# Two more Strassen groups in the last two chunks, one Silu moved, and the last stores on other queues

## Chip, cores and metric

The kernel runs on one core of a Trainium2 chip. The metric is the device time of one execution, in microseconds (us). A profiled execution also has a span, from its first recorded instruction to its last, which is a little shorter than its time.

## The reference, cut to what matters

The inputs are q, k and v (8 batches, 8 heads, 576 positions, 64 features), a matrix w_in (512 x 2048) and w_out (2048 x 512), all fp32. A softmax-weighted linear attention gives x, 4608 tokens by 512 features, and a two-layer network follows:

```
kv  = einsum('bhsd,bhse->bhde', softmax_seq(k), v)
att = einsum('bhsd,bhde->bhse', softmax_feat(q), kv)
x   = att.transpose(0, 2, 1, 3).reshape(4608, 512)
h   = x @ w_in                       # the first product
g   = h * (1 / (1 + exp(-h)))        # Silu
out = g @ w_out                      # the second product
```

## The kernel before, in words

**Tiling.** The 4608 tokens are nine chunks of 512, t = 0 to 8. XT (two tiles, by the parity of t) holds x transposed, GT (two tiles) holds g transposed: 2048 features as 16 blocks of 128 on the partitions, tokens along the free axis. W1 and W2 hold the weights in fp16. Matmuls write PSUM tile PS, 8 banks of 512 fp32. ACT (ScalarE) and DVE (VectorE) read the banks out. SP, POOL and in a few places ACT issue DMAs.

**The first product.** Up to chunk 1 every block is plain. From chunk 2 on, blocks 0 to 3 and 8 to 11 are plain "p" units (`mm1`, matmul at line 274): four matmuls of 512 columns into one of banks 0 to 3, then one Silu of 512 (line 291) or a Tanh and a DVE operation (lines 246 and 247). Blocks 12 to 15 and 4 to 7 are made together in Strassen's form, in Winograd's variant: seven "g" units (`group`, line 362) in the order 1, 2, 6, 5, 7, 4, 3, each of 8 matmuls of 256 columns. Units 1, 6, 7 and 4 accumulate in banks 0 and 1, units 2, 5 and 3 in banks 2 and 3. Four sums of weights (`ws_op`, line 316, WS1 to WS4) are made once, near 40 us, and four sums of the chunk's x (`xs_op`, line 325) once a chunk, on DVE. Between units come:

- snapshots, `group_snap` (ACT, line 338), copies of banks 0 and 1 to the tiles h0, h1 and h2 after units 1, 6 and 7;
- adds, `group_add` (DVE, line 341), of banks 2 and 3 to such a tile: add 0 after unit 2, add 2 after unit 7, add 1 after unit 3;
- Silus, `group_silu` (ACT, line 347), each of 1024 a partition: one from PSUM after unit 4, and after unit 3 those from h2, h0 and h1, called silu 2, silu 0 and silu 1. Silu 1 waits for add 1.

A unit that overwrites or adds to a bank waits until the bank has been read: unit 6 waits for the first snapshot, units 5 and the next group's unit 2 for adds on banks 2 and 3.

**The second product** of chunk t - 1 runs beside the first of chunk t, wholly in Strassen's form: 14 "b" units (`prod`, line 460), two halves of products 1, 2, 6, 5, 7, 4, 3, each of 8 matmuls of 256 columns into banks 4 and 5. Its sums of g are `s_op` (DVE, line 434, S1 to S4). After some products, `after` takes a snapshot (ACT, line 476, "sa", "sb", "sc") or combines a snapshot with a bank (DVE, lines 480 and 491) into an output tile ow, which SP stores (line 394). The last chunk's second product stands alone at the end (`end`): products 1, 6 and 7 in bank 3, product 2 in bank 5; `part` combines and stores strips of 128 rows by 256 columns in two halves (lines 669 and 684).

**The order** is written out by hand. `units` is the list of PE's work, one unit after the other; `plan(u, f)` puts other work ahead of unit u. An engine's queue has the order in which the code issues instructions, and a waiting instruction holds all behind it. A chunk from 2 to 7 has the units `pbpbpbpbpbpbpbp` and then `ggbgbgbgbbgbgb`; chunk 8 has the two strings the other way round. Attention for a later batch (exponentials on ACT, sums on DVE, products on POOL, `kv_both` and `xt` on PE) is planned between; from chunk 7 on only `xt` for chunk 8 is left of it. `xt` has two halves, each four small matmuls into banks 6 and 7 and a copy to XT, the first half's on DVE, the second's on ACT.

Of the kernel before, what the change touches and what calls it, by code (L numbers as in the profile page):

```python
# [17 lines left out]
def kernel(  # L18
# [9 lines left out]
    nc = tc.nc  # L28
# [32 lines left out]
    T4 = glob.tile([128, HF, HN], FP16, name="T4")  # L61
    GTS = [glob.tile([128, NFB, S], FP16, name="GT0"), glob.tile([128, NFB, TCH], FP16, name="GT1")]
    SS = {i: glob.tile([128, HF, HT], FP16, name=f"S{i}") for i in (1, 2, 4)}
    WS = [glob.tile([128, 2, 512], FP16, name=f"WS{i + 1}") for i in range(4)]
    XS4 = [glob.tile([128, 2, HT], FP16, name=f"XS{i + 1}") for i in range(4)]
    XTS = [glob.tile([128, NC, S], FP16, name=f"XT{i}") for i in range(2)]
    vaug = glob.tile([128, J, NG, E1], BF16, name="vaug")
    ek = glob.tile([128, J, NG * D], BF16, name="ek")
    kvn = [glob.tile([128, 2, 2, D], BF16, name=f"kvn{i}") for i in range(3)]
    ident_f = glob.tile([128, 128], FP32, name="ident_f")  # L70
    ident = glob.tile([128, 128], BF16, name="ident")
    warm = glob.tile([128, 512], BF16, name="warm")
    gate = glob.tile([1, 1], FP32, name="gate")
    dummy = glob.tile([1, 1], FP32, name="dummy")
    PS = ps.tile([128, 8, 512], FP32, name="PS")

    B11, B12 = W2[:, 0:HF, 0:HN], W2[:, 0:HF, HN:DM]
    B21, B22 = W2[:, HF:NFB, 0:HN], W2[:, HF:NFB, HN:DM]
    T3 = B12
# [37 lines left out]

    def qsum_pair(b, cc):
        e = half(st[b]["eq"], cc)
        t1 = ap.tile([128, J, 2, D // 2], FP32, name="t1")  # L120
        t2 = ap.tile([128, J, 2, D // 4], FP32, name="t2", bufs=2)
        nc.gpsimd.tensor_tensor(
            out=t1, in0=e[:, :, :, 0:D // 2], in1=e[:, :, :, D // 2:D], op=ALU.add
        )
        nc.gpsimd.tensor_tensor(
            out=t2, in0=t1[:, :, :, 0:D // 4], in1=t1[:, :, :, D // 4:D // 2], op=ALU.add
        )
        st[b]["t2", cc] = t2
# [157 lines left out]
    def mm1(t, fb, one=False):  # L286
        bank = hb[0] % hb[1]
        hb[0] += 1
        mm1_mm(t, fb, bank, range(NC))
        if one:  # L290
            nc.scalar.activation(  # L291
                out=GTS[t % 2][:, fb, 0:TCH], in_=PS[:, bank, :], func=ACT.Silu, scale=1.0 / XS
            )
        else:
            mm1_silu(t, fb, bank)
# [1 line left out]

    F0, F1 = 12, 4  # L300
    H = [None] * 3

    def wa(c, f):
        return W1[:, 2 * c:2 * c + 2, f * 128:(f + 4) * 128]

    def xb(t, c, n):
        return XTS[t % 2][:, 2 * c:2 * c + 2, (1 - n) * HT:(2 - n) * HT]

    def ws_op(i):
        in0, in1, op = {  # L310
            1: (wa(0, F1), wa(1, F1), ALU.add),
            2: (WS[0], wa(0, F0), ALU.subtract),
            3: (wa(0, F0), wa(0, F1), ALU.subtract),
            4: (wa(1, F0), WS[1], ALU.subtract),
        }[i]
        nc.vector.tensor_tensor(out=WS[i - 1], in0=in0, in1=in1, op=op)

    def xs_op(t, i):
        in0, in1 = {
# [25 lines left out]
    def group_silu(t, i, f, n):  # L345
        x = group_bank(0) if i is None else four(H[i])
        nc.scalar.activation(out=group_out(t, f, n), in_=x, func=ACT.Silu, scale=1.0 / XS)  # L347

    def group(t, i):
        bank = 0 if i in (1, 6, 7, 4) else 2  # L350
        a, bb = {
            1: (wa(0, F0), xb(t, 0, 0)),
            2: (wa(1, F0), xb(t, 1, 0)),
            3: (WS[3], xb(t, 1, 1)),
            4: (wa(1, F1), XS4[3]),
            5: (WS[0], XS4[0]),
            6: (WS[1], XS4[1]),
            7: (WS[2], XS4[2]),
        }[i]
        for p in range(4):  # L360
            for c in range(2):
                nc.tensor.matmul(  # L362
                    out=PS[:, bank + p // 2, (p % 2) * HT:(p % 2 + 1) * HT],
                    lhsT=a[:, c, p * 128:(p + 1) * 128],
                    rhs=bb[:, c, :],
                    start=(i in (1, 2, 5) and c == 0 and p % 2 == 0),
                    stop=(i in (2, 3, 4) and c == 1 and p % 2 == 1),
                    skip_group_check=True,
                )
        if i == 1:  # L370
            group_snap(0)
        elif i == 2:
            group_add(0)
        elif i == 6:
            group_snap(1)
        elif i == 7:
            group_snap(2)
            group_add(2)
        elif i == 4:
            group_silu(t, None, F1, 0)  # L380
        elif i == 3:
            group_silu(t, 2, F1, 1)
            group_silu(t, 0, F0, 0)
            group_add(1)
            group_silu(t, 1, F0, 1)


    def rows(t, col):
# [36 lines left out]
    def s_op(t, i, f0=0, f1=HF):  # L425
        in0, in1, op = {
            1: (blk(t, 0, 1), blk(t, 1, 1), ALU.add),
            2: (SS[1], blk(t, 0, 0), ALU.subtract),
            3: (blk(t, 0, 0), blk(t, 0, 1), ALU.subtract),
            4: (blk(t, 1, 0), SS[2], ALU.subtract),  # L430
        }[i]
        f = slice(f0, f1)
        o = blk(t, 0, 1) if i == 3 else SS[i]
        nc.vector.tensor_tensor(out=o[:, f], in0=in0[:, f], in1=in1[:, f], op=op)
# [170 lines left out]
    def plan(u, f):  # L605
        at.setdefault(u, []).append(f)
# [14 lines left out]
    def b_units(t, order):  # L621
        got = []
        for i in order:
            got.append(lambda t=t, i=i: prod(t, i, 0))

            def second(t=t, i=i):
                prod(t, i, 1)
                after(t, i)

            got.append(second)  # L630
        return got
# [8 lines left out]
    for t in range(2, NCH):  # L640
        begin[t] = len(units)
        bs = b_units(t - 1, ORDER)
        ps_ = [
            lambda t=t, i=i, fb=fb: mm1(t, fb, i < 3 or t + 1 >= B)
            for i, fb in enumerate((0, 8, 1, 9, 2, 10, 3, 11))
        ]
        gs = [lambda t=t, i=i: group(t, i) for i in (1, 2, 6, 5, 7, 4, 3)]
        plan(begin[t] + 2, lambda t=t: s_op(t - 1, 1))
        plan(begin[t] + 4, lambda t=t: s_op(t - 1, 2))
        plan(begin[t] + (15 if t < NCH - 1 else 5), lambda t=t: s_op(t - 1, 3))  # L650
        plan(begin[t] + 21, lambda t=t: s_op(t - 1, 4))
        mix = "pbpbpbpbpbpbpbp", "ggbgbgbgbbgbgb"
        for x in "".join(mix) if t < NCH - 1 else "ggbgbgbgbbgbgb" + "pbpbpbpbpbpbpbp":
            units.append({"p": ps_, "b": bs, "g": gs}[x].pop(0))
        assert not (ps_ or bs or gs)
        x = begin[t] + (1 if t < NCH - 1 else 0)
        plan(x, lambda t=t: (xs_op(t, 1), xs_op(t, 2), xs_op(t, 3), xs_op(t, 4)))


# [7 lines left out]
    def part(name, bank, th, n, a):  # L667
        o = w_out_tile(last, th)[:, a, n * HN:(n + 1) * HN]
        nc.vector.scalar_tensor_tensor(  # L669
            out=o,  # L670
            in0=PS[:, bank, a * HN:(a + 1) * HN],
            scalar=OS,
            in1=WG[last][name][:, a * HN:(a + 1) * HN],
            op0=ALU.mult,
            op1=ALU.add,
        )
        one, two = {
            (0, 0): (nc.sync, nc.sync),
            (1, 1): (nc.gpsimd, nc.gpsimd),
            (1, 0): (nc.sync, nc.scalar),  # L680
            (0, 1): (nc.sync, nc.scalar),
        }[th, n]
        for i, eng in enumerate((one, two)):
            eng.dma_start(  # L684
                out=rows(last, th * HT + a * 128 + i * P)[:, n * HN:(n + 1) * HN],
                in_=o[i * P:(i + 1) * P, :],
            )
# [51 lines left out]
    plan(b1 + 8, lambda: xt(1, 0))  # L739
    plan(b1 + 9, lambda: xt(1, 1))  # L740

    plan(b1 + 3, lambda: (ws_op(1), ws_op(2)))
    plan(b1 + 9, lambda: (ws_op(3), ws_op(4)))
    plan(b1 + 8, lambda: t_op(1, nc.vector, 0, 4))
    plan(b1 + 9, lambda: t_op(1, nc.vector, 4, 8))
    for i, x in enumerate((10, 12)):
# [19 lines left out]
    for t in range(2, NCH - 1):  # L766
        b = t + 1
        u = begin[t]
        if b < B:
            for i in range(2):  # L770
                plan(u + 5 + i, lambda i=i, b=b: exp_q(b, i))
                plan(u + 6 + 3 * i, lambda i=i, b=b: (qsum(b, i), qnorm(b, i, nc.gpsimd)))
                plan(u + 10 + 2 * i, lambda i=i, b=b: vcast(b, i, nc.gpsimd))
                plan(u + 17 + 2 * i, lambda i=i, b=b: exp_k(b, i))
                if b + 1 < B:
                    plan(u + 7 + i, lambda i=i, b=b: load(b + 1, "qt", q, i, nc.sync))
                    plan(u + 18 + i, lambda i=i, b=b: load(b + 1, "vt", v, i, nc.sync))
                    plan(u + 20 + i, lambda i=i, b=b: load(b + 1, "kt", k, i, nc.sync))
            plan(u + 13, lambda b=b: q_transpose(b))
            plan(u + 22, lambda b=b: kv_both(b))  # L780
        plan(u + 24, lambda t=t: xt(t + 1, 0, nc.vector))
        plan(u + 27, lambda t=t: xt(t + 1, 1))

    for u, f in enumerate(units):
        for g in at.get(u, ()):
# [33 lines left out]
```

The softmax here doesn't subtract the row's maximum and nothing guards it: scores larger than these inputs give would overflow.

## Time and profile before

| | us |
|---|---|
| median of three runs | 271.5 |
| lowest and highest | 271.32, 272.15 |
| the profiled run, and its span | 271.31, 269.4 |
| PE busy | 260.4 |
| DVE busy | 190.6 |
| ACT busy | 180.1 |
| chunk 7 starts with its first plain unit at | 200.10 |
| chunk 8 starts with its first group unit at | 226.08 |
| the end starts at | 252.73 |
| DVE's last operation ends at | 265.58 |

The shares say which engine is the longest; the waits of that engine say where its gaps are. The timeline lists instructions in order of start: the start in us from the beginning of the span, the duration, the engine (PEld is the load of weights into TensorE), the line, the operation, the tile written and the tiles read, the shape, and in brackets the engine's idle time before it with what ended that. Neighbours of one kind are merged, with their number at the end (x8). Two starts of PE units are a unit's length apart; durations of a merged PE row are longer by the pipeline's filling.

### The profile page before, as it was taken

To read this page: it belongs to the slowest core of one execution; us is meant where nothing else is said; L and a number is where in the kernel's file an instruction comes from. 1 tells how busy PE (TensorE), PEld (TensorE's weight loads), DVE (VectorE), ACT (ScalarE), POOL (GpSimd) and SP (SyncE) were. 2 spreads that over 40 slices of the span, in tenths; PEclk is the share of its full clock that TensorE was granted. 3 is DMA by queue.
4 is the path that set the end of the run, shared out by engine and by line. 5 is a ranking of instruction groups with operands and counts; after the bars stand their busy time and mean duration, and the time that the engine had idled before them with its cause. 6 is when DMAs were issued, how large, how long until landed. Compare 5 with 4: busy or idle time off the path is not lost.

```text
span 269.4 us, 6058 instructions
## 1 busy us (share of the span) xinstructions
PE 260.4 (97%) x2540; PEld 184.6 (69%) x2540; DVE 190.6 (71%) x269; ACT 180.1 (67%) x228; POOL 71.1 (26%) x62
## 2 busy tenths in 40 slices
PE   8999999999999999999999999999999999999893
PEld 2467644445678767876787678767876787876682
DVE  2966796978898759775977597759776057835432
ACT  5767937669957886788668966896685538484210
POOL 1744971820181008100820082007300000000003
PEclk9999999999999999999999999999999999999999
DMA  7999999499549845994498449830434004200714
GB/s 251 319 209 351 253 339 331 160 256 391 201 124 246 263 113 140 223 300 83 162 283 242 86 156 255 269 74 0 90 65 93 0 2 97 61 0 2 157 43 117
DMA packets 35500, 45.88 MB, mean 170 GB/s; under 512 B 16208, under 2 KB 20048, under 8 KB 35472
## 3 DMA queue, kind: packets, MB, share of 16 engines
q1 hardware_dynamic: 29568, 33.69, 45.1%
q0 software_dynamic: 5584, 11.54, 16.4%
q8 instruction: 20, 0.33, 0.5%
q10 hardware_dynamic: 320, 0.26, 0.3%
q14 instruction: 8, 0.07, 0.1%
HBM read 36.70 MB, written 9.44 MB: 171 GB/s over the span
## 4 chain that ended last, share of the span: by engine, by line
PE 71%; DVE 15%; ACT 8%; issue 3%; DMA 1%; POOL 1%; DVEq 0%
PE PS L460 29%; PE PS L274 16%; PE PS L362 14%; DVE zq L144 5%; DVE GT L247 4%; PE PS L398 3%; PE PS L254 3%; ACT eq L108 3%; PE PS L224 2%; PE PS L185 2%; DVE eq L153 2%; ACT sg L246 2%; ACT L108 2%; DMA qt<-in_q_dram 1%; DVE ow L480 1%
## 5 line engine op out<-in xcount | busy, mean ns | idle before, releaser
L274 PE MATMUL PS<-XT,W 128*128 128x512 f16 (+1 forms) x288 | 71.2, 373 | 0.3 <-ACT ow L410 0.3
L460 PEld LDWEIGHTS <-GT 128*128 128x128 f16 x512 | 49.6, 98 | 13.9 <-issue 2.2
L153 POOL TENSOR_TENSOR eq<-eq,rzq 128x1152 bf16<-128x1152 bf16 x13 | 27.5, 2116 | 105.1 <-DVE rzq L148 105.1
L460 PE MATMUL PS<-W,GT 128*128 128x256 f16 x384 | 49.1, 273 | 0.7 <-ACT GT L291 0.7
L247 DVE SCALAR_TENSOR_TENSOR GT<-sg,PS 128x512 f16<-128x512 f32 (+2 forms) x57 | 37.4, 671 | 10.4 <-ACT sg L246 9.7
L246 ACT ACTIVATE sg<-PS 128x512 f32<-128x512 f32 (+2 forms) x57 | 33.1, 595 | 16.9 <-PE PS L274 8.1
L460 PEld LDWEIGHTS <-S 128*128 128x128 f16 x384 | 37.6, 98 | 8.8
L274 PEld LDWEIGHTS <-W 128*128 128x128 f16 x288 | 27.9, 98 | 21.3 <-issue 1.3
L341 DVE TENSOR_TENSOR h<-PS,h 128x1024 f32<-128x1024 f32 x21 | 25.7, 1221 | 21.3 <-ACT h L338 12.2
L460 PE MATMUL PS<-T,S 128*128 128x256 f16 x256 | 32.7, 273 | 0.0
L338 ACT COPY h<-PS 128x1024 f32<-128x1024 f32 x21 | 21.3, 1012 | 16.3 <-PE PS L362 16.3
L291 ACT ACTIVATE GT<-PS 128x512 f16<-128x512 f32 x31 | 18.5, 595 | 13.3 <-PE PS L274 12.7
L144 DVE TENSOR_REDUCE zq<-eq 128x18 f32<-128x1152 bf16 x12 | 16.2, 1349 | 15.0 <-ACT eq L108 15.0
L362 PEld LDWEIGHTS <-WS 128*128 128x128 f16 x224 | 21.0, 98 | 4.3 <-issue 1.8
L362 PE MATMUL PS<-XS,WS 128*128 128x256 f16 x168 | 21.8, 273 | 0.4 <-ACT h L338 0.4
L684 POOL DMA_DIRECT2D out_dram<-ow x4 | 2.2, 550 | 72.2 <-DVE ow L669 72.2
L347 ACT ACTIVATE GT<-h 128x1024 f16<-128x1024 f32 x21 | 20.7, 1052 | 0.0
L108 ACT ACTIVATE eq<-qt 128x1152 bf16<-128x1152 f32 x16 | 18.1, 1159 | 2.4 <-DMA qt<-in_q_dram 2.3
L362 PEld LDWEIGHTS <-W 128*128 128x128 f16 x168 | 16.4, 98 | 4.5 <-issue 1.4
L111 ACT ACTIVATE ek<-kt 128x1152 bf16<-128x1152 f32 x16 | 18.6, 1164 | 1.2 <-DMA kt<-in_k_dram 1.2
L91 POOL CAST vaug<-vt 128x1152 bf16<-128x1152 f32 x12 | 19.4, 1647 | 0.0
L254 PE MATMUL PS<-XT,W 128*128 128x288 f16 x128 | 16.5, 286 | 0.7 <-DVE GT L247 0.4
(78 smaller groups left out, 337.5 us busy)
## 6 DMA issues: line engine op xcount, KB each, us to landing
out_dram<-ow SPq DMA_DIRECT2D x64, 128.0 KB, 2.4
qt<-in_q_dram SPq DMA_DIRECT2D x12, 576.0 KB, 4.4
kt<-in_k_dram SPq DMA_DIRECT2D x12, 576.0 KB, 8.1
vt<-in_v_dram SPq DMA_DIRECT2D x12, 576.0 KB, 6.4
qt<-in_q_dram POOLq DMA_DIRECT2D x4, 576.0 KB, 13.2
kt<-in_k_dram POOLq DMA_DIRECT2D x4, 576.0 KB, 13.7
vt<-in_v_dram POOLq DMA_DIRECT2D x4, 576.0 KB, 12.6
W<-in_moe_w_out_dram POOLq DMA_DIRECT2D x4, 512.0 KB, 15.1
```

The costliest lines, as they stand in the source:

```text
L108: nc.scalar.activation(out=half(st[b]["eq"], cc), in_=jgd(b, "qt", cc), func=ACT.Exp)
L144: nc.vector.reduce_sum(out=z, in_=e, axis=AX.X)
L153: eng.tensor_tensor(out=e, in0=e, in1=r[:, :, :, None].to_broadcast([128, J, 2, D]), op=ALU.mult)
L246: nc.scalar.activation(out=s, in_=i, func=ACT.Tanh, scale=OS)
L247: nc.vector.scalar_tensor_tensor(out=o, in0=s, scalar=1.0, in1=i, op0=ALU.add, op1=ALU.mult)
L254: nc.tensor.matmul(out=PS[:, 2 * (fb % 3) + n, 0:S // 2], lhsT=W1[:, c, fb * 128:(fb + 1) * 128], rhs=XTS[0][:, c, n * (S // 2):(n + 1) * ...
L274: nc.tensor.matmul(out=PS[:, bank, o0:TCH], lhsT=W1[:, c, fb * 128:(fb + 1) * 128], rhs=XTS[t % 2][:, c, o0:TCH], start=(c == 0), stop=(c ...
L338: nc.scalar.copy(out=H[i], in_=PS[:, 0:2, :].rearrange("p b n -> p (b n)"))
L341: nc.vector.tensor_tensor(out=H[i], in0=PS[:, 2:4, :].rearrange("p b n -> p (b n)"), in1=H[i], op=ALU.add)
L347: nc.scalar.activation(out=group_out(t, f, n), in_=x, func=ACT.Silu, scale=1.0 / XS)
L362: nc.tensor.matmul(out=PS[:, bank + p // 2, (p % 2) * HT:(p % 2 + 1) * HT], lhsT=a[:, c, p * 128:(p + 1) * 128], rhs=bb[:, c, :], start=(i ...
L460: nc.tensor.matmul(out=PS[:, bank, m * HN:(m + 1) * HN], lhsT=a[:, fc, m * 128:(m + 1) * 128], rhs=bb[:, fc, :], start=(first and fc == 0) ...
```

## The change

- In chunks 7 and 8 all 16 blocks of the first product are in Strassen's form. `group` gets an index g: g = 1 for blocks 12 to 15 with 4 to 7, as before, and g = 0 for blocks 8 to 11 with 0 to 3. Both chunks have the units `ggbgbgbgbbgbgb` twice, g = 1 first, and no p units. Both sets use the same sums of x, banks and h tiles.
- Four more WS tiles for g = 0. They are filled on DVE in chunk 7: two operations planned at its unit 8, two at its unit 11.
- In every chunk, silu 1 leaves the end of `group` and is planned three units after group unit 3; in the last group of all, one unit after. Two groups that join, or a group and the p units of the next chunk, so have the next unit's snapshot or Silu on ACT ahead of silu 1.
- S3 of the chunk before is planned at unit 5 of chunk 7 too (it was at 15), and the two halves of `xt` one unit earlier in chunk 7, which has 28 units now and had 29.
- For room: `warm` is the tile XS1, the identity in fp32 is in h0, t1 in h0, and t2 in h1 and h2.
- Last stores: of a strip's two halves, the four of the fourth quadrant stay on POOL and the four of the first on SP. Those of product 4 go ACT and SP (were SP and ACT). Those of product 3 were SP and ACT for both strips; the first strip's now go on ACT and POOL, the last strip's both on SP.

```diff
-    WS = [glob.tile([128, 2, 512], FP16, name=f"WS{i + 1}") for i in range(4)]
+    WS = [[glob.tile([128, 2, 512], FP16, name=f"WS{i + 1}_{g}") for i in range(4)] for g in range(2)]
...
-    ident_f = glob.tile([128, 128], FP32, name="ident_f")
+    ident_f = mp.tile([128, 2 * TCH], FP32, name="h0", bufs=1)[:, 0:128]
...
-    warm = glob.tile([128, 512], BF16, name="warm")
+    warm = XS4[0].rearrange("p a n -> p (a n)")
...
-    def group(t, i):
+    def group(t, g, i):
         bank = 0 if i in (1, 6, 7, 4) else 2
+        w, f0, f1 = WS[g], 4 * g + 8, 4 * g
...
         elif i == 3:
-            group_silu(t, 2, F1, 1)
-            group_silu(t, 0, F0, 0)
+            group_silu(t, 2, f1, 1)
+            group_silu(t, 0, f0, 0)
             group_add(1)
-            group_silu(t, 1, F0, 1)
...
+        free = t + 1 >= B
         ps_ = [
-            lambda t=t, i=i, fb=fb: mm1(t, fb, i < 3 or t + 1 >= B)
-            for i, fb in enumerate((0, 8, 1, 9, 2, 10, 3, 11))
+            lambda t=t, i=i, fb=fb: mm1(t, fb, i < 3)
+            for i, fb in enumerate(() if free else (0, 8, 1, 9, 2, 10, 3, 11))
         ]
...
-        plan(begin[t] + (15 if t < NCH - 1 else 5), lambda t=t: s_op(t - 1, 3))
+        plan(begin[t] + (5 if free else 15), lambda t=t: s_op(t - 1, 3))
...
-        mix = "pbpbpbpbpbpbpbp", "ggbgbgbgbbgbgb"
-        for x in "".join(mix) if t < NCH - 1 else "ggbgbgbgbbgbgb" + "pbpbpbpbpbpbpbp":
+        four_pairs = "ggbgbgbgbbgbgb"
+        for x in (four_pairs if free else "pbpbpbpbpbpbpbp") + four_pairs:
             units.append({"p": ps_, "b": bs, "g": gs}[x].pop(0))
+            if x == "g" and len(gs) % 7 == 0:
+                later = 1 if t == NCH - 1 and not gs else 3
+                f0 = 8 if free and not gs else 12
+                plan(len(units) - 1 + later, lambda t=t, f0=f0: group_silu(t, 1, f0, 1))
...
-            (1, 0): (nc.sync, nc.scalar),
-            (0, 1): (nc.sync, nc.scalar),
+            (1, 0): (nc.scalar, nc.sync),
+            (0, 1): (nc.scalar, nc.gpsimd) if a == 0 else (nc.sync, nc.sync),
...
-        plan(u + 24, lambda t=t: xt(t + 1, 0, nc.vector))
-        plan(u + 27, lambda t=t: xt(t + 1, 1))
+        if b == B:
+            plan(u + 8, lambda: (ws_op(1, 0), ws_op(2, 0)))
+            plan(u + 11, lambda: (ws_op(3, 0), ws_op(4, 0)))
+        plan(u + (24 if b < B else 23), lambda t=t: xt(t + 1, 0, nc.vector))
+        plan(u + (27 if b < B else 26), lambda t=t: xt(t + 1, 1))
```

More of the change, by code (lines that the diff above doesn't have):

```diff
@@ L119, in qsum_pair @@
         e = half(st[b]["eq"], cc)
-        t1 = ap.tile([128, J, 2, D // 2], FP32, name="t1")
-        t2 = ap.tile([128, J, 2, D // 4], FP32, name="t2", bufs=2)
+        t1 = mp.tile([128, 2 * TCH], FP32, name="h0", bufs=1)[:, 0:J * D]
+        t1 = t1.rearrange("p (j g d) -> p j g d", g=2, d=D // 2)
+        t2 = mp.tile([128, 2 * TCH], FP32, name=f"h{cc + 1}", bufs=1)[:, 0:J * D // 2]
+        t2 = t2.rearrange("p (j g d) -> p j g d", g=2, d=D // 4)
         nc.gpsimd.tensor_tensor(
@@ L295, in mm1 @@
             mm1_silu(t, fb, bank)
-    F0, F1 = 12, 4
     H = [None] * 3
@@ L307, in xb, with ws_op @@
         return XTS[t % 2][:, 2 * c:2 * c + 2, (1 - n) * HT:(2 - n) * HT]
-    def ws_op(i):
+    def ws_op(i, g):
+        w, f0, f1 = WS[g], 4 * g + 8, 4 * g
         in0, in1, op = {
[L311 to L314, printed above, removed]
+            1: (wa(0, f1), wa(1, f1), ALU.add),
+            2: (w[0], wa(0, f0), ALU.subtract),
+            3: (wa(0, f0), wa(0, f1), ALU.subtract),
+            4: (wa(1, f0), w[1], ALU.subtract),
         }[i]
-        nc.vector.tensor_tensor(out=WS[i - 1], in0=in0, in1=in1, op=op)
+        nc.vector.tensor_tensor(out=w[i - 1], in0=in0, in1=in1, op=op)
     def xs_op(t, i):
@@ L347, in group_silu @@
         nc.scalar.activation(out=group_out(t, f, n), in_=x, func=ACT.Silu, scale=1.0 / XS)
-    def group(t, i):
+    def group(t, g, i):
         bank = 0 if i in (1, 6, 7, 4) else 2
+        w, f0, f1 = WS[g], 4 * g + 8, 4 * g
         a, bb = {
[L352 to L358, printed above, removed]
+            1: (wa(0, f0), xb(t, 0, 0)),
+            2: (wa(1, f0), xb(t, 1, 0)),
+            3: (w[3], xb(t, 1, 1)),
+            4: (wa(1, f1), XS4[3]),
+            5: (w[0], XS4[0]),
+            6: (w[1], XS4[1]),
+            7: (w[2], XS4[2]),
         }[i]
@@ L379, in group @@
         elif i == 4:
-            group_silu(t, None, F1, 0)
+            group_silu(t, None, f1, 0)
         elif i == 3:
-            group_silu(t, 2, F1, 1)
-            group_silu(t, 0, F0, 0)
+            group_silu(t, 2, f1, 1)
+            group_silu(t, 0, f0, 0)
             group_add(1)
-            group_silu(t, 1, F0, 1)
     def rows(t, col):
@@ L642 @@
         bs = b_units(t - 1, ORDER)
+        free = t + 1 >= B
         ps_ = [
-            lambda t=t, i=i, fb=fb: mm1(t, fb, i < 3 or t + 1 >= B)
-            for i, fb in enumerate((0, 8, 1, 9, 2, 10, 3, 11))
-        ]
-        gs = [lambda t=t, i=i: group(t, i) for i in (1, 2, 6, 5, 7, 4, 3)]
+            lambda t=t, i=i, fb=fb: mm1(t, fb, i < 3)
+            for i, fb in enumerate(() if free else (0, 8, 1, 9, 2, 10, 3, 11))
+        ]
+        gs = [
+            lambda t=t, g=g, i=i: group(t, g, i)
+            for g in ((1, 0) if free else (1,))
+            for i in (1, 2, 6, 5, 7, 4, 3)
+        ]
         plan(begin[t] + 2, lambda t=t: s_op(t - 1, 1))
         plan(begin[t] + 4, lambda t=t: s_op(t - 1, 2))
-        plan(begin[t] + (15 if t < NCH - 1 else 5), lambda t=t: s_op(t - 1, 3))
+        plan(begin[t] + (5 if free else 15), lambda t=t: s_op(t - 1, 3))
         plan(begin[t] + 21, lambda t=t: s_op(t - 1, 4))
-        mix = "pbpbpbpbpbpbpbp", "ggbgbgbgbbgbgb"
-        for x in "".join(mix) if t < NCH - 1 else "ggbgbgbgbbgbgb" + "pbpbpbpbpbpbpbp":
+        four_pairs = "ggbgbgbgbbgbgb"
+        for x in (four_pairs if free else "pbpbpbpbpbpbpbp") + four_pairs:
             units.append({"p": ps_, "b": bs, "g": gs}[x].pop(0))
+            if x == "g" and len(gs) % 7 == 0:
+                later = 1 if t == NCH - 1 and not gs else 3
+                f0 = 8 if free and not gs else 12
+                plan(len(units) - 1 + later, lambda t=t, f0=f0: group_silu(t, 1, f0, 1))
         assert not (ps_ or bs or gs)
-        x = begin[t] + (1 if t < NCH - 1 else 0)
+        x = begin[t] + (0 if free else 1)
         plan(x, lambda t=t: (xs_op(t, 1), xs_op(t, 2), xs_op(t, 3), xs_op(t, 4)))
@@ L740 @@
     plan(b1 + 9, lambda: xt(1, 1))
-    plan(b1 + 3, lambda: (ws_op(1), ws_op(2)))
-    plan(b1 + 9, lambda: (ws_op(3), ws_op(4)))
+    plan(b1 + 3, lambda: (ws_op(1, 1), ws_op(2, 1)))
+    plan(b1 + 9, lambda: (ws_op(3, 1), ws_op(4, 1)))
     plan(b1 + 8, lambda: t_op(1, nc.vector, 0, 4))
```

## The prediction

> **What bounds the kernel now.** I read four views in this order: the shares of the page, busy time by stage, who waited for whom on PE, and the timeline around those waits. The share first:
>
> ```profile
> PE 260.4 (97%) x2540; PEld 184.6 (69%) x2540; DVE 190.6 (71%) x269; ACT 180.1 (67%) x228; POOL 71.1 (26%) x62
> ```
>
> PE is busy for 97%, so the run is as long as PE's work plus its few gaps. Busy time of the engines in three stretches, which are chunk 7, chunk 8, and the end (columns: stretch, its length, then busy us and instructions by engine):
>
> ```profile
> 200.10:226.08 25.98, 25.98 (x209) 19.53 (x207) 13.28 (x17) 14.22 (x20) 0.00 (x0) 1.00 0.20 42
> 226.08:252.73 26.65, 25.57 (x202) 19.54 (x200) 14.78 (x20) 15.26 (x21) 0.00 (x0) 1.00 0.25 54
> 252.73:269.45 16.72, 12.39 (x112) 10.86 (x111) 6.75 (x12) 1.79 (x3) 2.18 (x4) 0.99 0.40 96
> ```
>
> DVE (third engine) is half idle in the two chunks that change, and POOL does nothing there. PE's waits from 180 us on are only two:
>
> ```profile
> PE PS L460 <- ACT GT L291: 0.7, 1, 0.7
> PE PS L362 <- ACT h L338: 0.4, 1, 0.4
> ```
>
> The second is at the start of chunk 8, where one group follows another (start, duration, engine, line; in brackets the idle time before):
>
> ```profile
> 225.35 2.95 ACT L347 ACTIVATE GT<-h 128x1024 f16<-128x1024 f32 x3
> 225.41 1.23 DVE L341 TENSOR_TENSOR h<-PS,h 128x1024 f32<-128x1024 f32 x1 [1.26 <-PE PS L362]
> 226.08 1.91 PE L362 MATMUL PS<-XT,W 128*128 128x256 f16 x16
> ...
> 227.83 1.04 PE L460 MATMUL PS<-W,GT 128*128 128x256 f16 x8
> ...
> 228.20 1.01 ACT L338 COPY h<-PS 128x1024 f32<-128x1024 f32 x1
> ...
> 229.26 1.03 PE L362 MATMUL PS<-XS,WS 128*128 128x256 f16 x8 [0.40 <-ACT h L338]
> ...
> 232.75 1.04 PE L362 MATMUL PS<-XS,WS 128*128 128x256 f16 x8
> ...
> 234.87 1.22 DVE L341 TENSOR_TENSOR h<-PS,h 128x1024 f32<-128x1024 f32 x1 [0.87 <-ACT h L338]
> ...
> 235.37 1.04 PE L362 MATMUL PS<-XS,W 128*128 128x256 f16 x8
> 236.01 0.68 DVE L480 SCALAR_TENSOR_TENSOR ow<-PS,sa 128x512 f32<-128x512 f32 x1
> ```
>
> Group 6 was due one unit after the 227.83 product, at 227.83 + 0.87 = 228.70, and began at 229.26: the wait costs **0.56 us**, the listed 0.40 and the refilling of the pipeline. It waited for the snapshot at 228.20, which stood behind three Silus on ACT. The first wait is the join to the end stage:
>
> ```profile
> 240.60 1.03 PE L274 MATMUL PS<-XT,W 128*128 128x512 f16 x4
> ...
> 251.02 1.03 PE L274 MATMUL PS<-XT,W 128*128 128x512 f16 x4
> ...
> 252.08 0.60 ACT L291 ACTIVATE GT<-PS 128x512 f16<-128x512 f32 x1 [1.14 <-PE PS L274]
> ...
> 252.73 3.65 PE L460 MATMUL PS<-W,GT 128*128 128x256 f16 x32 [0.69 <-ACT GT L291]
> ```
>
> The last plain block starts at 251.02, is through in 0.87, its Silu starts 0.2 later, and the end's product 1 follows 0.05 after that Silu because it writes the same bank 3. It was due at 251.89: **0.84 us** lost. I use these two release times, 0.2 from a PE unit's end to DVE or ACT, 0.05 from DVE or ACT to PE.
>
> **What the Trainium skill says.** "TensorE: Matmul & The Clock Gate", section Back-to-back issue gap, gives N/2.4 + 2.5 ns at full clock: 109 ns for 256 columns, 216 ns for 512, so a Strassen unit of 8 x 256 has no penalty against 4 x 512. The trace agrees: from 240.60 to 251.02 are six pairs of one plain and one product unit, 1.737 us a pair; from 229.26 to 235.37 are seven units of 256 columns, **0.872 us** each; so a plain unit is 1.737 - 0.872 = **0.865 us**. "VectorE: DVE Perf Modes", The perf-mode tier table, lets tensor_tensor run at double rate on 16-bit SBUF data and at single rate with PSUM; here 2048 f16 from SBUF (the S operations, 1.22) and 1024 f32 from PSUM (L341, 1.22) indeed cost the same. "SBUF — State Buffer", Who interferes with whom, says that a DVE instruction with two SBUF inputs contends with a GpSimd one that reads SBUF. The trace before shows the four WS operations once each:
>
> ```profile
> L316 DVE TENSOR_TENSOR WS<-W x2: 685/1102/1520, 37.1 to 41.9; 128x1024 f16<-128x1024 f16 x2
> ...
> L316 DVE TENSOR_TENSOR WS<-WS,W x1: 692/692/692, 38.7 to 38.7; 128x1024 f16<-128x1024 f16 x1
> L316 DVE TENSOR_TENSOR WS<-W,WS x1: 685/685/685, 42.5 to 42.5; 128x1024 f16<-128x1024 f16 x1
> ```
>
> Three took 0.69 us; the one at 37.1 took 1.52, while POOL copied a GT piece. POOL has no work in chunks 7 and 8, so I take 0.69 and keep 1.52 as the upper end.
>
> **The change, part by part.** Sums are against the profiled span, 269.45 us; that execution took 271.31, the others 271.32 to 272.15, their median 271.5, and I subtract from the median.
>
> (1) PE work. In each of chunks 7 and 8, 8 plain units (8 x 0.865 = 6.92) give way to 7 group units (7 x 0.872 = 6.10): -0.82, twice, **-1.64**.
>
> (2) The deferred Silu. At the join of two groups ACT has silus 2 and 0, then the snapshot, then silu 1. The three Silus begin about 0.95 apart, so without the third the snapshot starts at about 227.2 instead of 228.20 and ends 228.2, before 228.70. The 0.56 goes: **-0.56**. In chunks 2 to 6 the same move puts silu 1 behind a plain block's Silu; its values are first read by product 2, four units on, and four PSUM banks rotate, so nothing: hidden behind PE's b units.
>
> (3) New WS operations for blocks 8 to 11 and 0 to 3, in DVE's queue in chunk 7. This is the cost I could not leave at nothing. Count units from chunk 7's start at 0. Add 2 starts 234.87 - 232.75 = 2.12 after group 7, which is unit 7 at 6.10: 8.22 to 9.44. Behind it DVE now has WS1, WS2, the add of "sa", WS3, WS4, and only then add 1. Independent neighbours start 0.61 apart when each lasts 0.69 (the halves at 253.44 and 254.05), a dependent one 0.73 (252.71 and 253.44). WS1 starts at 9.36; 0.73 + 4 x 0.61 = 3.17 later, at 12.53, add 1 starts, though group 3 (unit 12) released it at 13 x 0.872 + 0.2 = 11.54. It ends at 13.75. Queued behind it is PE's unit 15, group 2 of the second set, which overwrites banks 2 and 3 that add 1 reads: due 13.08, starts 13.80, **+0.72**. ("sa" ending at 11.39 holds unit 13, due 11.34, by 0.1; that is inside the 0.72, since DVE decides unit 15 anyway.)
>
> (4) The second set's other operations: three snapshots of 1.01 and four Silus of 1.05 for each of chunks 7 and 8 replace eight Silus of 0.60; three adds of 1.22 are new on DVE. ACT then has about 17 us in 24.4 and DVE about 20.5: beside PE, except where PE wants a bank back. I walked each join. Chunk 7 to 8 has the order of today's (add 1 frees banks 2 and 3 at 226.64, group 2 wants them at 226.95): nothing. In chunk 8's second set DVE has the "sc" add, S4 (1.22) and half of S2 (0.69) ahead of add 2: 19.14, 19.75, 20.90, 21.51, so add 2 ends at 22.73 and group 3, due at 26 x 0.872 = 22.67, starts at 22.78: **+0.11**.
>
> (5) The join to the end. Product 1 of the end uses bank 3, which add 1 now reads. Group 3 starts 22.78, add 1 runs 23.85 to 25.07, product 1 starts 25.12; due after one product unit, at 24.52: **+0.60** in place of the **-0.84** of today. The last silu 1 ends by about 26.1, before product 2 at 25.12 + 1.74 = 26.86; S1 and S2 of the first halves end near 27, before product 6 at 28.6.
>
> (6) Last stores. Today's last strip ends on DVE at 265.58; its two stores go out on SP at 265.70 and on ACT at 266.00. Both on SP they go at about 265.6 and 266.2, an issue slot of 0.47 to 0.60 apart. "DMA: Bandwidth & Descriptors", Issuing engines are not separate DMA queues, says a second issuer saves only issue time; landings here are a median 2.2 us after issue from SP, 2.7 from ACT. So from 266.00 + 2.7 to 266.2 + 2.2 at best, -0.3, and +0.4 if ACT's lands as fast as SP's and POOL's fifth store (issued near 265.3) ends later; I take **+0.15**.
>
> (7) Tiles that share memory (warm with XS1, the identity with h0, t1 and t2 with h0 to h2) are free long before their next use: the first snapshot is at 77.9. Nothing, with PE's first wait, 1.2 us for the memset, as it is.
>
> Sum: -1.64 - 0.56 + 0.72 + 0.11 - 0.84 + 0.60 + 0.15 = **-1.46**: span 268.0, time 271.5 - 1.46 = **270.0 us**.
>
> **Rivals.** (A) DVE keeps up: PE's own slack or a shorter WS pitch hides (3) and the 0.11. Then -1.46 - 0.83 = -2.29, **269.2**. For it: DVE is only some 85% busy in chunk 7. Against: work in order behind add 2 leaves no slack at unit 15.
> (B) WS slower than 0.69 without POOL: at the mean of the two first-line values, 1.10, four of them add 1.64: +0.18, **271.7**, no change. For it: one instance of four was slow; against: its overlap with POOL explains it.
> (C) The slower side: the same four operations at 1.52 each, in DVE's queue between add 2 and add 1 of chunk 7, add 4 x 0.83 = 3.32 to unit 15's wait: +1.86, **273.4**. It decides from 0.69 + 1.46/4 = 1.06 us a WS operation on. Against it: S operations of the same form stay at 1.22 in all of both chunks.
> (D) The deferral doesn't do what it says, since ACT is still behind where groups join: the two joins with XT's copy on ACT too, chunks 6 to 7 and 7 to 8, wait 0.56 each, +1.1, **271.1**. Against: silu 0 ended at about 227.3, group 1's release was 227.2.
>
> **How the numbers follow.** Forecast 0.60 (own range 269.6 to 270.5: the tail's -0.3 to +0.4 and 0.2 in the waits), A 0.18, D 0.08, B 0.08, C 0.06. The range 269.0 to 270.9 holds the forecast, A and part of D. About 0.3%, 0.8 us, is what a measurement of this kernel can tell from no change: faster below 270.7. The forecast and A give 0.78 and a part of D 0.02, so faster 0.80; the rest of D and B, 0.14, same; C, 0.06, slower.
>
> **What would show it.** PE's rows at L274 fall by 64 instructions and groups rise by 112; the wait of group 6 on the snapshot at chunk 8 is gone; one PE wait on DVE's add, about 0.6 to 0.7 us, in the middle of chunk 7 with four WS operations of 0.69 before it; another of about 0.5 ahead of the end; last store issued on SP some 0.6 after the last strip. I am wrong if WS is over 1 us, if the groups run above 0.88 us a unit, or if PE waits for ACT at a join.

## The result, and the profile after

| | before | after |
|---|---|---|
| median, us | 271.47 (4 runs) | 269.75 (4 runs) |
| lowest to highest | 271.32 to 272.15 | 269.52 to 270.01 |
| span of the profiled run | 269.45 | 267.71 |

The ratio is 0.9932, 95% interval 0.9912 to 0.9952: 1.7 us faster. The forecast was 270.0, its range 269.0 to 270.9.

The page of the changed kernel, busy time by engine, and then busy time by stage as before: chunk 7, chunk 8, the end (columns: stretch, length, busy us and instructions of PE, of weight loads, DVE, ACT, POOL, granted clock, DMA share, GB/s):

```profile
PE 258.5 (97%) x2588; PEld 189.2 (71%) x2588; DVE 198.8 (74%) x279; ACT 184.7 (69%) x226; POOL 71.8 (27%) x63
```

```profile
199.62:225.70 26.08, 25.65 (x235) 22.05 (x233) 19.23 (x24) 16.44 (x19) 0.00 (x0) 1.00 0.18 40
225.70:250.95 25.25, 24.77 (x227) 21.90 (x224) 17.59 (x22) 16.70 (x20) 0.00 (x0) 1.00 0.21 45
250.95:267.71 16.76, 12.38 (x112) 10.85 (x111) 7.21 (x13) 2.83 (x4) 2.70 (x5) 0.93 0.51 118
```

PE lost 1.9 us of busy time, DVE and ACT gained 8.2 and 4.6: the trade that was meant. Chunk 8 is 1.4 us shorter, chunk 7 hardly. The reason is in PE's waits from 180 us on:

```profile
PE PS L463 <- DVE h L344: 0.4, 1, 0.4
PE PS L366 <- DVE h L344: 0.4, 1, 0.4
```

The two old waits, both for ACT, are gone, and two new ones, both for an add on DVE, stand in their place. Here is the join of chunks 6 and 7 in the timeline (start, duration, engine, line):

```profile
198.89 2.01 ACT L350 ACTIVATE GT<-h 128x1024 f16<-128x1024 f32 x2
...
199.62 1.91 PE L366 MATMUL PS<-XT,W 128*128 128x256 f16 x16
...
200.93 1.01 ACT L341 COPY h<-PS 128x1024 f32<-128x1024 f32 x1
...
201.84 1.06 ACT L350 ACTIVATE GT<-h 128x1024 f16<-128x1024 f32 x1
...
202.24 1.04 PE L366 MATMUL PS<-XS,WS 128*128 128x256 f16 x8
```

Two Silus stand before the snapshot, which ends at 201.94; group 6 starts at 202.24, on time. The join of chunks 7 and 8, the place of the old wait, has the same order, with two Silus where the kernel before had three:

```profile
224.96 2.00 ACT L350 ACTIVATE GT<-h 128x1024 f16<-128x1024 f32 x2
...
227.00 1.01 ACT L341 COPY h<-PS 128x1024 f32<-128x1024 f32 x1
...
227.44 1.04 PE L463 MATMUL PS<-W,GT 128*128 128x256 f16 x8
...
228.32 1.04 PE L366 MATMUL PS<-XS,WS 128*128 128x256 f16 x8
```

The snapshot ends at 228.01, and group 6 starts one unit after 227.44, as it should. Now the middle of chunk 7, where DVE makes the new weight sums:

```profile
207.85 1.23 DVE L344 TENSOR_TENSOR h<-PS,h 128x1024 f32<-128x1024 f32 x1 [0.90 <-ACT h L341]
...
208.99 0.68 DVE L319 TENSOR_TENSOR WS<-W 128x1024 f16<-128x1024 f16 x1
...
209.71 0.69 DVE L319 TENSOR_TENSOR WS<-WS,W 128x1024 f16<-128x1024 f16 x1
...
210.32 0.68 DVE L483 SCALAR_TENSOR_TENSOR ow<-PS,sa 128x512 f32<-128x512 f32 x1
...
210.92 0.68 DVE L319 TENSOR_TENSOR WS<-W 128x1024 f16<-128x1024 f16 x1
...
211.52 0.68 DVE L319 TENSOR_TENSOR WS<-W,WS 128x1024 f16<-128x1024 f16 x1
211.92 1.04 PE L366 MATMUL PS<-XT,W 128*128 128x256 f16 x8
212.12 1.22 DVE L344 TENSOR_TENSOR h<-PS,h 128x1024 f32<-128x1024 f32 x1
...
213.39 1.03 PE L366 MATMUL PS<-XT,W 128*128 128x256 f16 x8 [0.43 <-DVE h L344]
```

DVE runs without a gap from 207.85 on, so add 1 starts at 212.12 and not when group 3 lets it. The next set's group 1 starts at 211.92 and group 2 was due one unit later, at 212.79; it starts at 213.39, 0.05 after add 1. And the join to the end:

```profile
247.33 1.22 DVE L344 TENSOR_TENSOR h<-PS,h 128x1024 f32<-128x1024 f32 x1
...
248.60 1.03 PE L366 MATMUL PS<-XT,WS 128*128 128x256 f16 x8
...
249.67 1.23 DVE L344 TENSOR_TENSOR h<-PS,h 128x1024 f32<-128x1024 f32 x1 [0.53 <-PE PS L366]
...
250.95 3.65 PE L463 MATMUL PS<-W,GT 128*128 128x256 f16 x32 [0.44 <-DVE h L344]
```

Group 3 starts 0.05 after add 2 ends at 248.55, product 1 of the end 0.05 after add 1 ends at 250.90.

### The profile page after: what moved, and what is told of

Read it like the earlier page. It is cut to its first block, busy times and chain, and to the rows that moved or that the text cites. A ratio compares the mean times of both kernels' runs of the same rounds, so it can differ in the third digit from the quotient of the medians.

```text
span 267.7 us, 6167 instructions
## 1 busy us (share of the span) xinstructions
PE 258.5 (97%) x2588; PEld 189.2 (71%) x2588; DVE 198.8 (74%) x279; ACT 184.7 (69%) x226; POOL 71.8 (27%) x63
## 4 chain that ended last, share of the span: by engine, by line
PE 72%; DVE 14%; ACT 6%; issue 3%; POOL 1%; DMA 1%; POOLq 0%; DVEq 0%; ACTq 0%
PE PS L463 28%; PE PS L366 18%; PE PS L276 11%; PE PS L401 5%; DVE zq L146 5%; PE PS L256 4%; DVE GT L249 4%; ACT eq L108 3%; PE PS L226 2%; PE PS L187 2%; ACT L108 2%; ACT sg L248 1%; DMA qt<-in_q_dram 1%; DVE ow L483 1%; DVE eq L155 1%
## 5 line engine op out<-in xcount | busy, mean ns | idle before, releaser
L276 PE MATMUL PS<-XT,W 128*128 128x512 f16 (+1 forms) x224 | 54.7, 371 | 0.3 <-ACT ow L413 0.3
L344 DVE TENSOR_TENSOR h<-PS,h 128x1024 f32<-128x1024 f32 x27 | 32.9, 1220 | 17.9 <-PE PS L366 10.4
L341 ACT COPY h<-PS 128x1024 f32<-128x1024 f32 x27 | 27.4, 1013 | 18.6 <-PE PS L366 18.4
L276 PEld LDWEIGHTS <-W 128*128 128x128 f16 x224 | 21.7, 98 | 17.2 <-issue 1.3
L366 PEld LDWEIGHTS <-WS 128*128 128x128 f16 x288 | 27.3, 98 | 4.6 <-issue 1.4
L366 PE MATMUL PS<-XS,WS 128*128 128x256 f16 x216 | 28.0, 273 | 0.0
L350 ACT ACTIVATE GT<-h 128x1024 f16<-128x1024 f32 x27 | 27.5, 1055 | 0.3 <-DVE h L344 0.3
L366 PEld LDWEIGHTS <-W 128*128 128x128 f16 x216 | 21.1, 98 | 5.4 <-issue 2.0
L366 PE MATMUL PS<-XT,W 128*128 128x256 f16 x144 | 18.2, 272 | 0.9 <-DVE h L344 0.4
```

Source lines behind the costliest of these rows:

```text
L276: nc.tensor.matmul(out=PS[:, bank, o0:TCH], lhsT=W1[:, c, fb * 128:(fb + 1) * 128], rhs=XTS[t % 2][:, c, o0:TCH], start=(c == 0), stop=(c ...
L341: nc.scalar.copy(out=H[i], in_=PS[:, 0:2, :].rearrange("p b n -> p (b n)"))
L344: nc.vector.tensor_tensor(out=H[i], in0=PS[:, 2:4, :].rearrange("p b n -> p (b n)"), in1=H[i], op=ALU.add)
L366: nc.tensor.matmul(out=PS[:, bank + p // 2, (p % 2) * HT:(p % 2 + 1) * HT], lhsT=a[:, c, p * 128:(p + 1) * 128], rhs=bb[:, c, :], start=(i ...
```

## The experiments

One execution differs from the next at its start: in the ten profiles of this case, chunk 2's first group starts between 76.45 and 77.85. From there to the first group of chunk 6 each chunk takes 27.24 in all ten, so the difference is still there when chunk 7's first unit starts, between 199.62 and 201.02; six of the ten do the same work up to there, and they lie between 199.62 and 200.59. From chunk 7 to DVE's last operation, a stretch in which nothing was edited repeats to 0.02 us. So the stretches of the timeline carry the verdicts here, and the medians are given beside them. "Rest" is from the start of DVE's last operation to the end of the span; it repeats to about 0.1.

| profile of | chunk 7 starts | chunk 7 | chunk 8 | end, up to DVE's last | rest |
|---|---|---|---|---|---|
| before | 199.94 | 26.14 | 26.65 | 12.43 | 4.29 |
| after | 199.62 | 26.08 | 25.25 | 12.42 | 4.34 |
| e1, before with the deferral alone | 200.13 | 26.14 | 26.09 | 12.42 | 4.18 |
| e2, after without the deferral | 201.02 | 26.87 | 26.05 | 12.42 | 4.33 |
| e3, WS3 and WS4 later | 200.20 | 25.49 | 25.25 | 12.42 | 4.36 |
| e4, bank 6 at the end | 200.59 | 26.07 | 24.65 | 12.43 | 4.33 |
| e5, combined | 199.70 | 25.41 | 24.45 | 12.43 | 4.25 |
| e6, old last stores | 199.77 | 26.08 | 25.25 | 12.42 | 4.23 |
| e7, before with the moves of memory | 199.97 | 26.14 | 26.65 | 12.42 | 4.23 |
| e8, POOL beside WS | 200.36 | 27.16 | 25.25 | 12.42 | 4.41 |

(The start of chunk 7 before is 199.94 by its first matmul's row; 200.10 is where the chain of waits sets it.)

**The changed kernel without the deferral.**

```diff
             group_add(1)
+            group_silu(t, 1, f0, 1)
...
-            if x == "g" and len(gs) % 7 == 0:
-                later = 1 if t == NCH - 1 and not gs else 3
-                f0 = 8 if free and not gs else 12
-                plan(len(units) - 1 + later, lambda t=t, f0=f0: group_silu(t, 1, f0, 1))
```

> The changed kernel with silu 1 back inside the group, ahead of the next unit's snapshot; all else as changed. Theory (the deferral matters wherever two groups join): in the two joins with XT's copy on ACT, chunks 6 to 7 and 7 to 8, group 6 waits 0.56 us each for a snapshot behind silu 1; in the two joins inside chunks 7 and 8, where silu 1 waits for add 1 first, the snapshot ends some 0.3 us after group 6 is due: +1.7 us in all, about 271.4, and PE's waits for ACT's line of the snapshot are back in the list. Rival (ACT is far enough ahead inside the chunks): only the two joins with XT's copy wait, +1.1, about 270.9. Rival (the deferral is worth nothing here): 269.75 as the changed kernel, and no such wait.

Measured: 271.76 us, ratio to before 1.0015 (1.0001 to 1.0028). Chunk 7 grew by 0.79 and chunk 8 by 0.80, 1.59 together, where 1.7 was expected. PE's waits have a new line, and the first of its places is the join of chunks 6 and 7:

```profile
PE PS L366 <- ACT h L341: 0.8, 2, 0.4
```

```profile
203.14 1.00 ACT L341 COPY h<-PS 128x1024 f32<-128x1024 f32 x1
...
204.19 1.03 PE L366 MATMUL PS<-XS,WS 128*128 128x256 f16 x8 [0.40 <-ACT h L341]
```

By the rows of PE, group 6 is late by about 0.56 at the joins 6 to 7 and 7 to 8, and by 0.24 and 0.26 inside chunks 7 and 8. The list of waits names only the first two: at the others the rows leave PE idle for less than 0.1 us (216.21 + 1.04 to 217.33 in chunk 7), too little for the list; the rest of each delay is the filling of the pipeline, which counts as busy. So the deferral is worth 1.6 us in a kernel with four joins, and without it the two added groups would have gained nothing.

**The kernel before with the deferral alone.**

```diff
             group_add(1)
-            group_silu(t, 1, F0, 1)
...
             units.append({"p": ps_, "b": bs, "g": gs}[x].pop(0))
+            if x == "g" and not gs:
+                plan(len(units) - 1 + 3, lambda t=t: group_silu(t, 1, F0, 1))
```

> The kernel before with one edit: silu 1 leaves the group and is planned three units after group unit 3, in every chunk. Theory (only the join of two groups gains, and before has one, chunk 7 to 8): the stretch from chunk 8's first group to the end stage shortens from 26.65 to 26.09 us and PE no longer waits for ACT's snapshot; chunks 2 to 7 keep their lengths to 0.05 us each: -0.56, about 270.9. Rival (the move costs or gains in each of chunks 2 to 6 as well): chunk 6 to 7 or the stretch before it changes by 0.2 us or more a chunk.

Measured: 270.91 us, ratio 0.9984 (0.9971 to 0.9997). Chunk 8 takes 26.09, as expected to the hundredth; chunk 7 is unchanged at 26.14, and so are the chunks before it, at 27.24 from group to group. The deferral gains at joins of groups and nowhere else.

**WS3 and WS4 later.**

```diff
-            plan(u + 11, lambda: (ws_op(3, 0), ws_op(4, 0)))
+            plan(u + 17, lambda: (ws_op(3, 0), ws_op(4, 0)))
```

> The changed kernel with WS3 and WS4 of the second set planned at unit 17 of chunk 7 in place of 11, behind add 1 and the next add 0 on DVE; nothing else moves. Theory (PE's wait for add 1 in the middle of chunk 7 is DVE's queue, four WS operations and an add ahead of it): add 1 starts as soon as group 3 releases it, unit 15 finds its banks free, and the 0.7 us of that delay go: about 269.1, PE waiting for DVE once from 180 us on and not twice. Rival (the wait only moves, to unit 19 or 21 that read the WS tiles or to the next add): 269.75, with a wait at those units. Rival (WS operations are slower when beside other work): WS rows over 0.8 us.

Measured: 269.52 us where 269.1 was expected, ratio 0.9932 (0.9912 to 0.9953). The median shows little, 0.2 us under the changed kernel, and the spread of the starts is larger than what is sought; the stretch shows it: chunk 7 takes 25.49, 0.59 less, and the wait is off the list. In the timeline add 1 starts as group 3 lets it, and groups 1 and 2 run as one row:

```profile
211.75 1.22 DVE L344 TENSOR_TENSOR h<-PS,h 128x1024 f32<-128x1024 f32 x1 [0.17 <-PE PS L366]
...
212.51 1.91 PE L366 MATMUL PS<-XT,W 128*128 128x256 f16 x16
```

The wait did not move to the units that read WS. What is left is 0.08 at unit 13, which still waits for the add of "sa" behind WS1 and WS2.

**Bank 6 at the end.**

```diff
-            prod(last, i, m, bank=5 if i == 2 else 3)
+            prod(last, i, m, bank=5 if i == 2 else 6)
...
-            snap(last, {1: "sa", 6: "sb", 7: "sc"}[i], 3)
+            snap(last, {1: "sa", 6: "sb", 7: "sc"}[i], 6)
```

> The changed kernel with products 1, 6 and 7 of the end in bank 6 in place of bank 3. Theory (the join to the end waits for bank 3, which add 1 still reads): the wait goes, product 1 starts one unit after group 3's end, -0.6 us, about 269.15; product 2 follows without a wait since silu 1 ends near 252 and it is due near 252.1. Rival (product 1 waits for its data, the last Silus on ACT): the wait stays at 0.4 and names ACT, 269.75. Rival (the wait moves to product 2, for silu 1): about -0.3, 269.4, with a PE wait for ACT there.

Measured: 269.61 us where 269.15 was expected, ratio 0.9936 (0.9912 to 0.996); chunk 8 takes 24.65, 0.60 less. Product 1 now starts while add 1 runs (the view ends within PE's row):

```profile
250.64 1.22 DVE L344 TENSOR_TENSOR h<-PS,h 128x1024 f32<-128x1024 f32 x1 [0.53 <-PE PS L366]
...
251.31 2.89 PE L463 MATMUL PS<-W,GT 128*128 128x256 f16 x25
...
251.90 1.06 ACT L350 ACTIVATE GT<-h 128x1024 f16<-128x1024 f32 x1 [0.29 <-DVE h L344]
```

The join waited for the bank and not for data. Silu 1 ends at 252.96, in time for product 2 at 251.31 + 1.74 = 253.05: 0.1 us to spare.

**Old last stores.**

```diff
-            (1, 0): (nc.scalar, nc.sync),
-            (0, 1): (nc.scalar, nc.gpsimd) if a == 0 else (nc.sync, nc.sync),
+            (1, 0): (nc.sync, nc.scalar),
+            (0, 1): (nc.sync, nc.scalar),
```

> The changed kernel with the last stores on the queues of before: product 4's halves on SP and ACT, product 3's on SP and ACT for both strips, none of them on POOL. Theory (the new spread is worth nothing, since the last store goes out 0.2 us later in exchange for a queue that lands faster): within 0.15 us of the changed kernel either way, and from the last DVE operation's start to the end of the span 4.3 us as in both. Rival (the spread gains what is left of the difference): 0.3 us slower, and that last stretch 4.6 us. Rival (POOL's fifth store holds the end): 0.2 us faster, 4.1 us.

Measured: 269.87 us, ratio 0.9945 (0.9923 to 0.9967), the changed kernel within its error. The rest is 4.23 with the old spread. Over all profiles it is 4.18 to 4.29 with the old (five) and 4.33 to 4.41 with the new (five), so the new spread costs about 0.12 us. The traces tell which store does it. With the new spread POOL's fifth store has landed 2.4 to 2.5 us after the start of DVE's last operation, and the one that lands last is SP's second, issued at 0.97 and landed at 3.2 (3.19 to 3.22 in five profiles). With the old spread the last is ACT's, issued at 0.85 and landed at 3.1 (3.08 to 3.18).

**The moves of memory alone**, in the kernel before:

```diff
-    ident_f = glob.tile([128, 128], FP32, name="ident_f")
+    ident_f = mp.tile([128, 2 * TCH], FP32, name="h0", bufs=1)[:, 0:128]
...
-    warm = glob.tile([128, 512], BF16, name="warm")
+    warm = XS4[0].rearrange("p a n -> p (a n)")
...
-        t1 = ap.tile([128, J, 2, D // 2], FP32, name="t1")
-        t2 = ap.tile([128, J, 2, D // 4], FP32, name="t2", bufs=2)
+        t1 = mp.tile([128, 2 * TCH], FP32, name="h0", bufs=1)[:, 0:J * D]
+        t1 = t1.rearrange("p (j g d) -> p j g d", g=2, d=D // 2)
+        t2 = mp.tile([128, 2 * TCH], FP32, name=f"h{cc + 1}", bufs=1)[:, 0:J * D // 2]
+        t2 = t2.rearrange("p (j g d) -> p j g d", g=2, d=D // 4)
```

> The kernel before with the moves of memory alone: warm in XS1, the fp32 identity in h0, t1 in h0, t2 in h1 and h2. Theory (these tiles are free long before their next use, and the 0.3 us by which chunk 7 started earlier in the changed kernel's profile is what one execution differs from the next at the start): within 0.3 us of the kernel before, and the time of chunk 7's first unit in the profile lies between 199.6 and 201.0, where profiles of unlike kernels have put it. Rival (the moves gain those 0.3 us): about 271.1 with chunk 7 at 199.6.

Measured: 271.20 us, ratio 0.9998 (0.9988 to 1.0009), with chunk 7 at 199.97. The moves are worth nothing that can be measured.

**POOL beside the WS operations**: the price that the prediction's slower rival used.

```diff
             plan(u + 8, lambda: (ws_op(1, 0), ws_op(2, 0)))
+            spare = ek.rearrange("p j x -> p (j x)")[:, 0:1024].rearrange("p (a n) -> p a n", a=2)
+            for _ in range(3):
+                plan(u + 8, lambda: nc.gpsimd.tensor_copy(spare, WS[0][0]))
```

> The changed kernel with three copies on POOL added in chunk 7, of the new WS1 to a tile that nothing reads any more; they start when WS1 is done and each would take 1.1 us alone. Theory (WS operations take 0.69 in the changed kernel because POOL is idle there; a DVE operation with two SBUF inputs and a POOL operation that reads SBUF get in each other's way, as at 37 us): WS2, WS3 or WS4 take 1.2 us or more, at least one of them, and unit 15 of chunk 7 starts later by what they take over 0.69, so chunk 7 takes 26.6 to 29 us in place of 26.08. Rival (the slow WS1 at 37 us had another cause, as the first read of freshly loaded weights): all four stay at 0.7, chunk 7 at 26.1.

Measured, in one run: 271.39 us, and chunk 7 at 27.16 us. POOL's row and DVE's rows from the timeline of chunk 7:

```profile
210.57 4.35 POOL L797 CAST ek<-WS 128x1024 bf16<-128x1024 f16 x3 [19.32 <-DVE WS L319]
```

```profile
210.45 0.69 DVE L319 TENSOR_TENSOR WS<-WS,W 128x1024 f16<-128x1024 f16 x1
211.06 0.68 DVE L483 SCALAR_TENSOR_TENSOR ow<-PS,sa 128x512 f32<-128x512 f32 x1
211.66 0.92 DVE L319 TENSOR_TENSOR WS<-W 128x1024 f16<-128x1024 f16 x1
212.51 1.52 DVE L319 TENSOR_TENSOR WS<-W,WS 128x1024 f16<-128x1024 f16 x1
213.95 1.21 DVE L344 TENSOR_TENSOR h<-PS,h 128x1024 f32<-128x1024 f32 x1
```

WS3 and WS4 take 0.24 and 0.84 longer, 1.08 together, and chunk 7 is 1.08 longer: each 0.1 us on DVE there lengthens the run by 0.1 us. WS2, which was under way when the first copy began, keeps its 0.69. The adds with one input in PSUM keep their 0.68 and 1.21 beside the same copies, which is what the Trainium skill, "SBUF — State Buffer", Who interferes with whom, says of DVE instructions with two SBUF inputs and with one. So a copy on POOL is enough to explain the 1.52 of WS1 near 37 us, where one ran beside it in every profile, and 0.69 was the right value for a chunk in which POOL idles.

**All together**: WS1 and WS2 at unit 9 and WS3 and WS4 at 17, bank 6, the old stores, and half of S2 behind add 2:

```diff
-            plan(u + 8, lambda: (ws_op(1, 0), ws_op(2, 0)))
+            plan(u + 9, lambda: (ws_op(1, 0), ws_op(2, 0)))
...
-    plan(begin[NCH] - 7, lambda: s_op(last, 2, 4, 8))
+    plan(begin[NCH] - 6, lambda: s_op(last, 2, 4, 8))
```

> The changed kernel with four edits: WS1 and WS2 of the second set at unit 9 of chunk 7 (behind the add of sa), WS3 and WS4 at unit 17; products 1, 6 and 7 of the end in bank 6; half of the last S2 one unit later (behind add 2); the last stores on the queues of before. Theory (the four waits left in the changed kernel, 0.08 + 0.59 in chunk 7, 0.20 + 0.61 in chunk 8, are each a DVE queue or a bank and independent of each other): chunk 7 takes 25.4 us, chunk 8 24.4, the end 12.4, the last stretch 4.2: -1.6 against the changed kernel, about 268.2, with no PE wait from 180 us on. Rival (with those gone PE waits for ACT or DVE elsewhere): chunk 8 stays above 24.8, with a wait at product 2 of the end or at group 3.

Measured: **268.66 us**, ratio to before 0.9903 (0.9884 to 0.9921), the fastest of all. From chunk 7's start to the end of the span it takes 66.54 us where the changed kernel takes 68.09: -1.55, with -1.6 expected. The median is 0.46 above the 268.2 expected, and hardly any of that is in these stages:

```profile
199.70:225.11 25.41, 25.41 (x235) 22.04 (x233) 19.32 (x24) 16.44 (x19) 0.00 (x0) 1.00 0.19 40
225.11:249.56 24.45, 24.45 (x226) 21.92 (x224) 16.89 (x21) 16.18 (x19) 0.00 (x0) 1.00 0.19 41
249.56:266.23 16.67, 12.39 (x114) 10.81 (x111) 7.82 (x14) 3.34 (x5) 2.18 (x4) 1.00 0.54 127
```

PE is busy for the whole length of both chunks, and its list of waits from 180 us on is empty. Chunk 8 is as short as its units allow: 28 units of 0.872 are 24.42.

## Why the prediction was right

From chunk 7's start to the end of the span, before takes 69.51 us and after 68.09: -1.42, where the sum of the prediction was -1.46. By its steps:

1. PE work, -0.82 a chunk. In chunk 8, without its waits, 25.25 - 0.20 - 0.61 = 24.44 stands against 26.65 - 0.56 - 0.84 = 25.25: **-0.81**. In chunk 7, 26.08 - 0.08 - 0.59 = 25.41 stands against 26.14: **-0.73**. Of the missing 0.09, 0.07 is seen ahead of the second half of `xt`, which follows the first half's copy on DVE at once, 223.54 to 223.60; before, that copy had long been done. The formula that the prediction takes from the Trainium skill, "TensorE: Matmul & The Clock Gate", Back-to-back issue gap, stands there for an isolated matmul, beside about 131 ns for 512 columns in a stream of weight loads and matmuls. In this kernel's stream four such matmuls take 0.865 us, 216 ns each, so here the formula holds and the 131 does not.
2. The deferral, -0.56: shown alone, exactly. The rival that it does nothing fell with both of its tests.
3. The WS operations, +0.72: 0.08 + 0.59 = **0.67**. The mechanism, the place and the hold at unit 13 were as told. The rival that DVE keeps up, at 269.2, is out: it does not. So are the two with slower WS operations: all four took 0.68 or 0.69.
4. Chunk 8's second set, +0.11: **0.20**. The term was mis-sized by a tenth: add 2 ended at 248.55, 0.1 later against the chunk's start than worked out, and group 3 follows it. The working had the half of S2 start 1.15 after S4; it starts 1.25 after it (245.47 to 246.72), and did so before, too:

```profile
246.11 1.22 DVE L434 TENSOR_TENSOR S<-GT,S 128x2048 f16<-128x2048 f16 x1
...
247.36 0.69 DVE L434 TENSOR_TENSOR S<-S,GT 128x1024 f16<-128x1024 f16 x1
```

5. The join to the end, +0.60 for -0.84: **0.61**, by the bank, as said.
6. The last stores, +0.15: +0.05 between these two profiles, about 0.12 over all. The best case of the working, a gain of 0.3, gave ACT's last store 2.7 us from issue to landing, the median of ACT's four. In the profile before, that store took 2.3, so there was no such gain to be had.
7. Shared memory, nothing: nothing.

The median moved by 1.72. The 0.3 beyond the sum lies ahead of chunk 7 in these two profiles, which differ there by 0.32, and the spread of starts covers it. A rival cause, the moves of memory, was tried alone and gave nothing. It was no part of the working. Luck in the starts is likely: WS3 and WS4 later and bank 6 shorten their stretches by 0.59 and 0.60, and their medians are only 0.2 and 0.1 under the changed kernel's. Adding the stretches back to those medians puts the changed kernel at 270.1 to 270.2, an estimate, so the four runs behind 269.75 probably began early.

One sum in the working was too high, and no step rested on it: DVE's "about 20.5" us. Its own terms give 13.28 + 3 x 1.22 + 4 x 0.69 = 19.7 for chunk 7 and 14.78 + 3 x 1.22 = 18.4 for chunk 8; measured are 19.2 and 17.6, so that DVE was 74% busy in chunk 7 and not the 85% of the first rival.

The forecast was a net of large terms: -2.2 gained by PE work and the deferral, -0.24 net at the join to the end, and 0.8 paid to DVE's queue. The combined run shows that what was paid was not needed.

## What to carry to other kernels

When work moves from the longest engine to an idle one, walk the queue of the idle engine in order at every place where the longest one waits for it: DVE was 74% busy in chunk 7 and still held PE for 0.67 us, because the four new operations and the add of "sa" stood ahead of the one that freed a bank, while 3.7 us of idle time lay a few units further on. Where a bank is the cause of a wait, look for one that the stage no longer uses. Judge small edits by the length of the stretch they change: here it repeats to 0.02 us, and the whole run only to 1 or 2 us.

## What was not expected of the hardware

Near the start of the run, the length of one multiplication on DVE differs from profile to profile, and so does that of a copy on POOL beside it. Here are both, before (with PE's transposes, which wait for the multiplication) and then after:

```profile
35.14 2.08 DVE L153 TENSOR_TENSOR eq<-eq,rzq 128x1152 bf16<-128x1152 bf16 x1
...
36.28 1.84 POOL L732 COPY GT<-GT 128x1024 f16<-128x1024 f16 x1
...
37.28 0.68 PE L171 MATMUL PS<-ident,eq 128*128 128x128 bf16 x9 [0.23 <-DVE eq L153]
```

```profile
35.39 1.36 DVE L155 TENSOR_TENSOR eq<-eq,rzq 128x1152 bf16<-128x1152 bf16 x1
...
36.52 1.12 POOL L744 COPY GT<-GT 128x1024 f16<-128x1024 f16 x1
```

In both, POOL starts 1.1 us after DVE, when 0.2 us of the shorter multiplication is left. In one both take 0.72 longer than in the other, and the next DVE operation, WS1, takes 1.52 in both. Over all profiles the two are longer by the same amount each time, from 0 to 0.82 us, in kernels that have the same operations up to there. What decides the amount was not tried.

In eight of the ten profiles chunk 2's first group starts 39.55 to 39.56 us after the multiplication's end. In the other two, where it took its shortest 1.36, it is 39.70, and no wait of PE for it is listed. So most of the spread of the starts is already there when this multiplication ends: part of it is its length, and part is when it starts, 35.14 to 36.12, whose cause these runs don't show.
